# Conformer block on one core: attention outputs summed in two turns instead of in two banks with a reduce

## The chip, the cores and the metric

The kernel runs on one core of one Trainium2 chip. The metric is the device time of one execution in microseconds. PE is TensorE, the matrix engine, whose results land in PSUM (eight banks of 512 float32 for each of 128 partitions). ScalarE (ACT) computes functions such as the exponential, VectorE (DVE) does elementwise work and reductions, GpSimd (POOL) takes small work, and SP issues DMAs. Each engine works its own list of instructions in order, and the engines meet at semaphores: an instruction that waits holds everything behind it on its engine.

## The reference

Input x has 2 sequences of 4000 tokens with 144 features. One Conformer block is computed: a feed-forward half step, attention with 4 heads of 36 features, a gated convolution over 5 tokens, a second feed-forward half step, and a layer norm ahead of each part and at the end.

```
h = layernorm(x);  x = x + 0.5 * silu(h @ w_ff1a) @ w_ff1b
h = layernorm(x);  q, k, v = split(h @ w_qkv)                 # 4 heads of 36
p = softmax(q @ k.T * 36**-0.5);  x = x + (p @ v) @ w_o      # 4000 x 4000 for each head
h = layernorm(x) @ w_pw1;  h = h[:, :144] * sigmoid(h[:, 144:])
x = x + silu(conv5(h, dw)) @ w_pw2
h = layernorm(x);  x = x + 0.5 * silu(h @ w_ff2a) @ w_ff2b
return layernorm(x)
```

The attention is by far the most work: 2 x 4 heads x 4000 x 4000 exponentials, all of which have to leave PSUM through ScalarE or VectorE.

## The kernel before

Tokens are cut into 16 chunks of 512 (the last of each sequence has 416). The attention runs over 32 groups; a group is one chunk of queries and one pair of heads (`groups`). For each group there are 31 tiles of 128 keys, and a rest of 32 keys that is done for four heads at once (`rest`). A tile goes like this:

- Scores (`scores`): for both heads, and for each half of the 128 keys, one matmul on a 64 x 64 quadrant of PE. Four such matmuls run side by side and fill two banks. Two pairs of banks (0 to 3) take turns, so that the scores of a tile wait for the exponential of the tile two before.
- Exponential (`emit_exp`): one ScalarE instruction reads two banks and writes a PT buffer (1024 values a row, bf16). There are `NPT` PT buffers.
- Some tiles go to VectorE instead (`far_tiles`, and single heads in `emit_exp`): a linear instruction writes a 16-bit pattern to a PU buffer, and four more (`exact`, with the buffers PF and PC) correct it to an exponential. There are `NPD` PU buffers.
- Outputs (`outputs`, called by `emit_O`, `bits_outputs` and `rest`): for both heads and each half of the keys a quadrant matmul with the values (36 columns and a column of ones, which gives the softmax's denominator). The two halves of the keys sit on different row halves of PE and add into different banks: keys 0 to 63 of every tile into bank 4, keys 64 to 127 into bank 5, each for all 512 queries.
- At the end of a group the epilogue adds the two banks with one `tensor_reduce` on VectorE into the tile OTF (float32), PE transposes OTF, and VectorE divides. The first output of the next group has to wait until the banks are read.

Banks 6 and 7 are for everything else. While one group runs, the other parts of the block (layer norms, feed-forward, projections, convolution) of other chunks run between its tiles.

The order of the work is written by a planner in the kernel's Python code, at build time. `Rec` records every instruction with an estimated cost, keeps an estimated free time for each engine, and adds the latencies `LAT` from an instruction to the ones that need it. `Sched` holds threads (generators) which ask for an engine or a buffer; it runs the one that can start first, and among those within a tolerance the one with the best rank. The main loop at the end takes a thread or the next tile, whichever can start first. Numbers that steer it are in `TUNE`, one set for each eighth of the 32 groups: how free VectorE must be before it takes one head, how many tiles must be left before one goes to VectorE, how near GpSimd may be, the tolerance, and when a correction is hurried. `Rec.finish` turns the recorded dependences into semaphore waits. It leaves out dependences of PE on PE, as PE works in order.

All instructions are issued from one helper (line 163), so the profile's groups are told apart by the names of the tiles: PT, PU, PF, PC, OTF as above, QT and KT queries and keys, VA values, PS the PSUM banks, and DUM the zeros of filler matmuls.

Of the kernel before, what the change touches and what calls it, by code (L numbers as in the profile page):

```python
# [13 lines left out]
DH = 36  # L14
# [23 lines left out]
class Rec:  # L38
# [5 lines left out]
    LAT = dict(pe=0.195, act=0.243, dve=0.152, pool=0.08, sp=3.0)  # L44
# [14 lines left out]
    def op(self, eng, name, *a, r=(), w=(), q=None, cost=0.1, kind=None, lat=None, port=False, **k):  # L59
# [10 lines left out]
        for key in w:  # L70
            h = self.hist.setdefault(key, ([], []))
            o.deps += [(d, False) for d in h[0] + h[1] if d is not o]
            if h[1] and not (len(h[1]) == 1 and h[1][0] is o):
                self.hist[key] = ([o], [])
            else:
                h[0].append(o)
        start = self.free[eng]
        for d, raw in o.deps:
            if d.eng != eng or d.q is not None or (raw and eng != "pe"):
                start = max(start, d.done - self.NEAR.get((d.eng, eng), 0.0))  # L80
# [28 lines left out]
    def finish(self, group_qs=()):  # L109
        eng_clock = {e: {} for e in self.ENGS}  # L110
        for o in self.ops:
            clk = eng_clock[o.eng]
            need = {}
            for d, raw in o.deps:
                lane = d.eng if d.q is None else "q:" + d.q
                if d.q is None and d.eng == o.eng and (d.eng == "pe" or not raw or o.q is not None):
# [184 lines left out]
def bass_standalone__conformer_family_zipformer__speech_kernel(  # L301
# [35 lines left out]
    NPT, NPD, NUS, NQS = 7, 3, 7, 10  # L337
# [4 lines left out]
    TUNE = [(0.003, 10, 0.47, 0.032, 3), (0.003, 10, 0.47, 0.032, 3), (0.003, 10, 0.47, 0.032, 3), (0.025, 10, 0.56, 0.065, 3), (0.089, 13, 0.66, 0.057, 3), (0.003, 10, 0.47, 0.032, 3), (0.022, 10, 0.67, 0.039, 3), (0.075, 12, 0.7, 0.063, 3)]  # L342
# [30 lines left out]
    PF = sb("PF", [NPD, 2, CH], U16)  # L373
    PC = sb("PC", [NPD, 2, CH])
# [121 lines left out]
    def fill_start(until):  # L496
# [6 lines left out]
        Slots(R, range(n)) for n in (NXN, NXT, NTH, NTB, NHT, NSW, 2, 2, NPD))  # L503
    mode = {"front": True, "tail": False}
# [426 lines left out]
    an_of = {}  # L931

    def epilogue(b, qc, p, gi):
# [46 lines left out]
    def output_flags(gi, bk, hh):  # L980
        first = (gi, bk, hh) not in begun
        begun.add((gi, bk, hh))
        return dict(start=first, stop=o_left[gi] == 1, skip_group_check=True)

    def outputs(gi, terms, rk):

        n = wid(gi // 2)
        for t in range(max(map(len, terms))):
            for r, (m0, m1) in enumerate(halves):
                for hh in range(2):  # L990
                    if t < len(terms[hh]):
                        v, w = terms[hh][t]
                        op("pe", "matmul", PSV[64 * hh:64 * hh + DH + 1, 4 + r, 0:n], lhsT=v[m0:m1, 0:DH + 1],
# [321 lines left out]
```

## Time and profile before

| what | value |
|---|---|
| time, median of 3 runs | 934.28 us (934.25 to 934.55) |
| profiled execution, its time | 935.62 us |
| profiled execution, span from first to last instruction | 933.8 us |
| granted PE clock | 1.00 |
| exponential instructions on ScalarE (PT) | 848 |
| corrections on VectorE (PC from PF) | 155 |
| reduces into OTF | 32, 38.4 us |

The page's first part has the busy time of each engine. Its fifth part has the groups of instructions: how many, their busy time in all, the mean of one, and the idle time of the engine just before them with what ended it. The means of one instruction overlap with the next one's start, so start-to-start times from the timeline or the chain are shorter than they. The chain of work runs back from the last instruction to whatever released it, and so on; its shares say which engine set the pace.

### The profile page before, as it was taken

What the parts mean: (1) busy time and instruction counts of PE and PEld (TensorE: products, weight loads), DVE (VectorE), ACT (ScalarE), POOL (GpSimd) and SP (SyncE); (2) the same over time, 40 slices, a digit from 0 to 9 for tenths busy, and PEclk for the clock granted to TensorE, in tenths of its full rate; (3) what the DMA queues carried; (4) which work ended last, traced back from release to release, by engine and by line L of the source; (5) the groups of instructions that cost most, each with busy time, mean ns of one, the idle gap of its engine ahead of it and who ended that gap; (6) DMA issues with size and microseconds to landing.
All of it is one profiled execution on the core that took longest, in us unless ns stands there. A gap on an engine that the chain in (4) does not pass through costs nothing.

```text
span 933.8 us, 25544 instructions
## 1 busy us (share of the span) xinstructions
PE 860.8 (92%) x10838; PEld 343.0 (37%) x10838; DVE 858.4 (92%) x1975; ACT 884.2 (95%) x1126; POOL 170.8 (18%) x395
## 2 busy tenths in 40 slices
PE   8998899999999998999999999899988999899989
PEld 5633233333243333334343333333323333333447
DVE  8868999999999999999989999999999999898954
ACT  6799999999999999999999999999999999999963
POOL 7500010302111120211211111102202120130223
DMA  5310010103011020201100020101001020101100
GB/s 143 50 21 13 13 25 13 40 8 46 13 28 27 7 52 14 38 16 24 28 8 5 16 36 11 30 7 30 20 1 30 13 42 2 30 18 22 22 19 14
DMA packets 79810, 23.26 MB, mean 25 GB/s; under 512 B 77120, under 2 KB 79696, under 8 KB 79696
## 3 DMA queue, kind: packets, MB, share of 16 engines
q1 hardware_dynamic: 78656, 21.15, 11.6%
q8 instruction: 85, 1.39, 0.7%
q10 hardware_dynamic: 1040, 0.48, 0.2%
q14 instruction: 29, 0.24, 0.1%
HBM read 3.31 MB, written 2.30 MB: 6 GB/s over the span
## 4 chain that ended last, share of the span: by engine, by line
ACT 60%; PE 25%; DVE 13%; DMA 1%; issue 1%; POOL 1%; SPq 0%; ACTq 0%; DVEq 0%
ACT PT L163 52%; PE PS L163 25%; ACT TH L163 5%; DVE PU L163 4%; DVE PC L163 2%; DVE XN L163 1%; DVE ST L163 1%; DVE X L163 1%; ACT HT L163 1%; DVE HT L163 1%; DVE PF L163 1%; DVE OTF L163 1%; ACT PR L163 1%; DMA XT<-XN 0%; POOL RS L163 0%
## 5 line engine op out<-in xcount | busy, mean ns | idle before, releaser
L163 ACT ACTIVATE PT<-PS 128x1024 bf16<-128x1024 f32 (+2 forms) x848 | 795.8, 1067 | 9.7 <-PE PS L163 7.1
L163 PE MATMUL PS<-QT,KT 64*64 64x512 bf16 (+1 forms) x4032 | 431.1, 389 | 49.4 <-ACT PT L163 36.1
L163 PE MATMUL PS<-PT,VA 64*37 64x512 bf16 (+1 forms) x3350 | 327.1, 371 | 0.8 <-ACT PT L163 0.6
L163 PEld LDWEIGHTS PS<-QT,KT 64*64 64x64 bf16 x4032 | 128.2, 103 | 325.2 <-ACT PT L163 199.9
L163 DVE TENSOR_SCALAR PU<-PS 128x512 uint16<-128x512 f32 (+1 forms) x309 | 201.4, 671 | 5.8 <-PE PS L163 4.2
L163 POOL TENSOR_SCALAR RS<-ST 128x2 f32<-128x2 f32 (+1 forms) x160 | 33.2, 208 | 689.8 <-DVE ST L163 688.8
L163 POOL TENSOR_TENSOR RS<-RS,NHALF 128x2 f32<-128x2 f32 (+1 forms) x160 | 122.5, 766 | 13.3
L163 DVE TENSOR_TENSOR PC<-PC,PF 128x1024 bf16<-128x1024 bf16 (+1 forms) x155 | 103.4, 671 | 0.6
L163 DVE TENSOR_TENSOR PU<-PU,PC 128x1024 uint16<-128x1024 uint16 (+1 forms) x155 | 103.4, 669 | 0.2
L163 PEld LDWEIGHTS PS<-PT,VA 64*37 64x37 bf16 x3350 | 96.5, 96 | 13.5 <-ACT PT L163 1.3
L163 DVE TENSOR_SCALAR XN<-X,ST,RS 128x144 bf16<-128x144 bf16 (+1 forms) x312 | 83.2, 311 | 12.9 <-POOL RS L163 11.8
L163 ACT ACTIVATE TH<-PS 128x512 bf16<-128x512 f32 (+2 forms) x135 | 88.7, 657 | 1.9 <-PE PS L163 1.8
L163 PE MATMUL PS<-XT,WA 128*128 128x512 bf16 (+3 forms) x256 | 71.1, 378 | 6.7 <-DVE PU L163 3.4
L163 DVE BATCH_NORM_STATS2 ST<-X 128x6 f32<-128x288 bf16 (+1 forms) x160 | 69.1, 449 | 0.6 <-DMA X<-in_x_dram 0.3
L163 DVE SCALAR_TENSOR_TENSOR HT<-TH,PS 128x512 bf16<-128x512 bf16 (+3 forms) x105 | 64.8, 618 | 3.8 <-ACT TH L163 3.5
L163 PE MATMUL PS<-PU,VA 64*37 64x512 bf16 (+1 forms) x618 | 66.8, 376 | 1.1 <-DVE PU L163 0.8
L163 DVE SCALAR_TENSOR_TENSOR X<-PS,X 128x288 bf16<-128x288 f32 (+1 forms) x128 | 56.1, 450 | 9.9 <-PE PS L163 8.9
L163 DVE TENSOR_SCALAR PC<-PF 128x1024 bf16<-128x1024 uint16 (+1 forms) x155 | 63.0, 411 | 0.3
L163 DVE TENSOR_SCALAR PF<-PU 128x1024 uint16<-128x1024 uint16 (+1 forms) x155 | 62.5, 412 | 0.1
L163 PE MATMUL PS<-WB,HT 128*128 128x144 bf16 (+1 forms) x640 | 56.1, 228 | 2.0 <-ACT HT L163 0.6
L163 PEld LDWEIGHTS PS<-WB,HT 128*128 128x128 bf16 (+1 forms) x640 | 39.7, 101 | 35.3 <-issue 19.3
L163 DVE TENSOR_REDUCE OTF<-PS 128x512 f32<-128x1024 f32 (+1 forms) x32 | 38.4, 1199 | 12.6 <-PE PS L163 12.3
(97 smaller groups left out, 600.5 us busy)
## 6 DMA issues: line engine op xcount, KB each, us to landing
X<-in_x_dram SPq DMA_DIRECT2D x14, 144.0 KB, 3.7
out_dram<-XN SPq DMA_DIRECT2D x28, 72.0 KB, 1.8
XT<-XN SPq DMA_TRANSPOSE x94, 2.5
XT<-AN SPq DMA_TRANSPOSE x28, 2.5
X<-in_x_dram SPq DMA_DIRECT2D x2, 117.0 KB
out_dram<-XN SPq DMA_DIRECT2D x4, 58.5 KB
WA<-in_w_ff1a_dram ACTq DMA_DIRECT2D x1, 144.0 KB, 2.8
WB<-in_w_ff1b_dram ACTq DMA_DIRECT2D x1, 144.0 KB, 3.9
```

What stands on the lines that cost most here:

```text
L163: ins = getattr(eng, o.name)(*o.a, **o.k)
```

## The change

- An output matmul now takes 256 of the 512 queries. Bank 4 belongs to queries 0 to 255 and bank 5 to queries 256 to 511, and both halves of the keys add into the same bank. So that the two row halves of PE do not write the same bank together, the outputs of a tile come in two turns: in turn 0 the upper keys' row half works on the other bank than the lower keys' half, in turn 1 they swap (`a = r ^ ph`). Each turn has four matmuls of 256 columns in place of four of 512.
- A turn's first matmul waits by semaphore for the last matmul of the other turn (`sync`, which `finish` keeps although both are on PE). The turn may change only after scores or other work has come between (`may`, `turn`); where nothing else is left, a filler matmul is put in (`apart`). Tiles whose turn 0 is done are kept in the list `half`; several tiles can share a turn.
- The banks then hold whole sums, and the epilogue copies 512 values instead of reducing 1024. The epilogue is now a thread that asks for VectorE once the banks are ready, and the next group's outputs begin after the copy is recorded (`copied`).
- There are 8 PT buffers instead of 7, 4 PU buffers instead of 3, and 2 PF and PC buffers instead of 3, in a pool of their own (`pfp`).
- The planner's latencies and the eight sets in `TUNE` have other values.

```diff
-    LAT = dict(pe=0.195, act=0.243, dve=0.152, pool=0.08, sp=3.0)
+    LAT = dict(pe=0.214, act=0.254, dve=0.145, pool=0.08, sp=3.0)
...
-    NPT, NPD, NUS, NQS = 7, 3, 7, 10
+    NPT, NPD, NUS, NQS = 8, 4, 7, 10
+    NPF = 2
...
-    TUNE = [(0.003, 10, 0.47, 0.032, 3), (0.003, 10, 0.47, 0.032, 3), (0.003, 10, 0.47, 0.032, 3), (0.025, 10, 0.56, 0.065, 3), (0.089, 13, 0.66, 0.057, 3), (0.003, 10, 0.47, 0.032, 3), (0.022, 10, 0.67, 0.039, 3), (0.075, 12, 0.7, 0.063, 3)]
+    TUNE = [(0.013, 10, 0.53, 0.033, 2), (0.013, 10, 0.53, 0.033, 2), (0.013, 10, 0.53, 0.033, 2), (0.013, 10, 0.53, 0.033, 2), (0.05, 10, 0.68, 0.043, 3), (0.08, 12, 0.56, 0.04, 3), (0.013, 10, 0.53, 0.033, 2), (0.013, 10, 0.53, 0.033, 2)]
...
-        op("dve", "tensor_reduce", out=OTF[:, 0:n], in_=PSV[:, 4:6, 0:n].rearrange("p b n -> p n b"),
-           axis=mybir.AxisListType.X, op=ALU.add, r=[("ps", 4), ("ps", 5)], w=["OTF"],
-           cost=dve_cost(2 * n))
+        yield need("dve", rank=free_first)
+        op("dve", "tensor_copy", OTF[:, 0:n].rearrange("p (a n) -> p a n", a=2),
+           PSV[:, 4:6, 0:n // 2], r=["po"], w=["OTF"], cost=dve_cost(n))
+        copied[gi] = R.last
...
+    def may(ph):
+        return R.kind != "q" or turn[0] in (None, ph)
+
+    def outputs(gi, ph, terms, rk, rows=(0, 1)):
...
+        turn[0] = ph
+        other = last_out[1 - ph]
+        for r in rows:
+            m0, m1 = halves[r]
+            a = r ^ ph
+            for hh in range(2):
+                if terms[hh] is not None:
+                    v, w = terms[hh]
+                    last_out[ph] = op(
+                        "pe", "matmul", PSV[64 * hh:64 * hh + DH + 1, 4 + a, 0:n // 2], lhsT=v[m0:m1, 0:DH + 1],
+                        rhs=w[m0:m1, a * n // 2:(a + 1) * n // 2], r=rk, w=["po"],
+                        cost=0.107 / ((terms[0] is not None) + (terms[1] is not None)) / len(rows), kind="q",
+                        sync=other, **output_flags(gi, 4 + a, hh, ph))
+                    other = None
...
-            S.add(epilogue(*groups[gi], gi), first=True)
+            S.add(epilogue(*groups[gi], gi), R.ready("po"), first=True)
...
     def emit_pending(force=False):
-        while pend:
+        if half and may(1):
+            for m in half:
+                emit_O(m, 1)
+            half.clear()
+        while pend and may(0):
...
+            emit_O(m, 0)
+            half.append(pend.pop(0))
+
+    def apart():
+        if turn[0] is None or not banks.free:
+            return False
+        i = min(banks.free)
+        op("pe", "matmul", PSV[:, i, 0:128], lhsT=DUM[:, 0:128], rhs=DUM[:, 0:128], start=True, stop=True, r=["DUM"],
+           w=[("ps", i)], cost=0.058, kind="f")
+        turn[0] = None
+        return True
```

More of the change, by code (lines that the diff above doesn't have):

```diff
@@ L978, in bass_standalone__conformer_family_zipformer__speech_kernel, with output_flags @@
     begun = set()
-    def output_flags(gi, bk, hh):
+    def output_flags(gi, bk, hh, ph):
         first = (gi, bk, hh) not in begun
         begun.add((gi, bk, hh))
-        return dict(start=first, stop=o_left[gi] == 1, skip_group_check=True)
-    def outputs(gi, terms, rk):
-        n = wid(gi // 2)
[L988 to L993, printed above, removed]
-                           rhs=w[m0:m1, 0:n], r=rk, w=[("ps", 4 + r)], cost=0.0535 if all(terms) else 0.107,
-                           kind="q", **output_flags(gi, 4 + r, hh))
+        return dict(start=first, stop=ph == 1 and o_left[gi] == 1, skip_group_check=True)
+    turn = [None]
+    last_out = [None, None]
+    def may(ph):
+        return R.kind != "q" or turn[0] in (None, ph)
+    def outputs(gi, ph, terms, rk, rows=(0, 1)):
+        n = wid(gi // 2)
+        assert may(ph)
+        turn[0] = ph
[12 more added lines that the diff above has]
+                    other = None
     def output_done(gi, n=1):
@@ L1058, in begun_group @@
     def begun_group(gi):
[L1059 removed]
+        return any((gi, bk, hh) in begun for bk in (4, 5) for hh in range(2))
     def close_pair():
```

91 lines of the change are left out of this document (54 added, 37 removed).

## The prediction

> **What bounds the kernel now.** I read the page's table of engines, then the groups of instructions, then the chain of work, and for single handovers the timeline.
>
> ```profile
> span 933.8 us, 25544 instructions
> PE 860.8 (92%) x10838; PEld 343.0 (37%) x10838; DVE 858.4 (92%) x1975; ACT 884.2 (95%) x1126; POOL 170.8 (18%) x395
> q8 instruction: 85, 1.39, 0.7%
> ```
>
> This is the share of busy time over the whole span. Three engines are at 92 to 95%, so one more view is needed: the middle stretch alone, where attention runs, as busy time by engine.
>
> ```profile
> 75.00:890.00 815.00, 750.57 (x9580) 275.87 (x9578) 779.38 (x1730) 803.31 (x993) 128.22 (x290) 1.00 0.11 21
> ```
>
> From 75 to 890 us the columns are PE, weight loads, VectorE, ScalarE, GpSimd: ScalarE is busy 803.3 of 815 us (98.6%), VectorE 779.4 (95.6%), PE 750.6, with PE's clock granted in full (1.00). The chain of work of the same stretch says who sets the pace:
>
> ```profile
> by line: ACT PT L163 58.5%; PE PS L163 18.6%; ACT TH L163 6.1%; DVE PU L163 5.1%; DVE PC L163 2.1%; DVE XN L163 0.9%; issue 0.8%; DVE HT L163 0.8%; DVE PF L163 0.8%; DVE OTF L163 0.8%; DVE X L163 0.6%; ACT PR L163 0.6%; DVE ST L163 0.6%; DM
> ```
>
> The reader should see that the exponentials on ScalarE (PT) are most of it, that PE has 18.6% (152 of 815 us, in bursts), and that OTF, the work that the change replaces, has only 0.8% (6.5 us) itself. So little is gained directly. Indirectly more can be: the planner moves exponential tiles from ScalarE to VectorE as VectorE has room, so time freed on VectorE becomes time on ScalarE. These are the groups that this runs over:
>
> ```profile
> L163 ACT ACTIVATE PT<-PS 128x1024 bf16<-128x1024 f32 (+2 forms) x848 | 795.8, 1067 | 9.7 <-PE PS L163 7.1
> L163 PE MATMUL PS<-PT,VA 64*37 64x512 bf16 (+1 forms) x3350 | 327.1, 371 | 0.8 <-ACT PT L163 0.6
> L163 PE MATMUL PS<-PU,VA 64*37 64x512 bf16 (+1 forms) x618 | 66.8, 376 | 1.1 <-DVE PU L163 0.8
> L163 DVE TENSOR_SCALAR PC<-PF 128x1024 bf16<-128x1024 uint16 (+1 forms) x155 | 63.0, 411 | 0.3
> L163 DVE TENSOR_REDUCE OTF<-PS 128x512 f32<-128x1024 f32 (+1 forms) x32 | 38.4, 1199 | 12.6 <-PE PS L163 12.3
> ```
>
> **Term 1, the reduce becomes a copy.** The reduce reads two banks (1024 values a row); the copy reads 512 and writes the same 512 float32. There is no such copy in the trace; the nearest rows move 512 or 416 float32 values of PSUM to SBUF.
>
> ```profile
> L163 DVE TENSOR_REDUCE OTF<-PS 128x512 f32<-128x1024 f32 x28 | 34.3, 1224 | 8.2 <-PE PS L163 8.0
> L163 DVE CAST KT<-PS 128x512 bf16<-128x512 f32 x25 | 17.2, 686 | 6.6 <-PE PS L163 6.6
> L163 DVE CAST QT<-PS 128x416 bf16<-128x416 f32 x4 | 2.3, 584 | 0.0
> L163 DVE TENSOR_REDUCE OTF<-PS 128x416 f32<-128x832 f32 x3 | 3.1, 1025 | 0.8 <-PE PS L163 0.8
> ```
>
> 28 x (1224 - 686) + 4 x (1025 - 584) ns = 15.1 + 1.8 = 16.8 us of VectorE less. Only the output type differs (bf16 in the row); I take the row.
>
> **Term 2, VectorE's wait before it.** The old reduce is put into VectorE's order as soon as the last output matmul is planned, and VectorE stands 12.6 us in all before it. In the new code the epilogue is a thread that becomes ready when the planner holds the banks for done, and other VectorE work can be put ahead. In the middle stretch it looks like this (us in total, times, longest):
>
> ```profile
> DVE OTF L163 <- PE PS L163: 8.8, 24, 0.7
> ```
>
> The other 3.5 us of the page's 12.3 are one wait at the end of the last group, where VectorE has nothing to put ahead. Bounds: 0 to 9.1 us given back; I take 6, as the waits are short and regular, of a kind that the planner's times resolve. Terms 1 and 2 together: 22.8 us of VectorE (bounds 16.8 and 25.9).
>
> **Term 3, what that buys.** One tile that moves takes from ScalarE one exponential and gives VectorE six instructions. Busy means overlap, so I take start-to-start steps, from the chain in order of time:
>
> ```profile
> 399.23 6.42 ACT PT L163 x7
> 418.40 1.20 DVE PU L163 x2
> 419.60 0.34 DVE PC L163
> 419.93 0.33 DVE PF L163
> 420.26 0.60 DVE PC L163
> 420.86 0.60 DVE PU L163
> ```
>
> ScalarE: 6.42 / 7 = 0.917 us a tile. VectorE: 1.20 + 0.34 + 0.33 + 0.60 + 0.60 = 3.07 us (the two conversions, the two tensor_scalars, the product and the sum). With both engines ending together, 22.8 us free let x tiles move with 3.07x + 0.917x = 22.8: x = 5.7, and ScalarE's end comes 5.2 us earlier. With 16.8 us it is 4.2 tiles and 3.9 us, with 25.9 us 6.5 tiles and 6.0 us; if none move, 0. I take 5.2. The more PU buffers (3 to 4) let a fourth such tile be open; PF and PC drop from 3 to 2, which costs nothing as VectorE runs one such chain at a time or two.
>
> **Term 4, the handover between groups.** The next group's first output must wait for the banks to be read. In the timeline of one handover (start, us, engine):
>
> ```profile
> 404.12 0.45 PE L163 MATMUL PS<-PT,VA 64*37 64x512 bf16 x4
> ...
> 404.62 1.23 DVE L163 TENSOR_REDUCE OTF<-PS 128x512 f32<-128x1024 f32 x1 [0.35 <-PE PS L163]
> ...
> 405.94 0.60 PE L163 MATMUL PS<-PT,VA 64*37 64x512 bf16 x8
> ```
>
> The last outputs start at 404.12 and the next ones at 405.94; between them stands the 1.23 us reduce. A 0.69 us copy takes 0.54 us off; against that the last tile's second turn comes one score step later. I book the direct part only: OTF's 0.8% of the chain is 6.5 us, of which 0.54/1.23 would go, 2.9 us; half of it is lost to the second turn: 1.4 us. One more PT buffer (7 to 8) only makes up for tiles held longer between their two turns; ScalarE's 7.1 us of waits on PE before PT are all that it could win or double. I book 0 (bounds -3 to +7).
>
> **Term 5, PE's price.** Output matmuls go from 512 to 256 columns: 3350 + 618 = 3968 become 7936, so the 992 sets of four become 1984 sets; the 32-row rest goes from 64 to 128. The columns streamed stay the same. What a step of a short set costs beyond streaming is seen in the convolution's quadrant matmuls:
>
> ```profile
> 400.20 0.41 PE L163 MATMUL PS<-QT,KT 64*64 64x512 bf16 x4
> 400.44 0.39 PE L163 MATMUL PS<-PT,VA 64*37 64x512 bf16 x4
> 400.66 0.38 PE L163 MATMUL PS<-QT,KT 64*64 64x512 bf16 x2
> ...
> 303.42 0.60 PE L163 MATMUL PS<-UA,DG 64*64 64x384 bf16 x8
> ```
>
> ```profile
> L163 PE MATMUL PS<-UA,DG 64*64 64x256 bf16 x112 | 12.1, 272 | 0.0
> ```
>
> From 400.44 to 400.66 a set of 512 columns takes 0.22 us, so 768 columns should take 0.33. By the code the eight convolution matmuls are four pairs of 384, 128, 256 and 256 columns. The last pair lasts 0.27 us, so the three steps before it, 768 columns, take 0.60 - 0.27 = 0.33 us: no overhead within the 0.03 us of rounding. A step costs at most 0.01 us beyond its columns, and I take that: 992 more steps, 10 us of PE. [...]
>
> Then the new wait. Before each change of turn PE waits for its own last output matmul of the other turn. The trace has no wait of PE on PE. From below it is 0: a set of scores lies between the turns, and PE often stands before those scores anyway, long enough for any matmul to end:
>
> ```profile
> PEld PS L163 <- ACT PT L163: 201.2, 425, 1.3
> ```
>
> From above: the outputs at 404.12 last 0.45 us where a set lasts 0.39, so the last of them began at some 404.18, and the waiting reduce started at 404.62, 0.44 us on. The columns take 0.22 us, so completion trails them by 0.22. A set of scores between hides that (0.24 us, 400.20 to 400.44); without one, all 0.22 is lost. I take 0.02 us, the 0.41 against 0.39 us that a set takes when its weights were not loaded ahead; about one turn per ScalarE tile, 848 x 0.02 = 17 us. Behind a waiting output on PE stand the next scores, and behind those the next exponential. PE's 10 + 17 = 27 us count where PE is in the chain, 18.6%: 5.0 us. But a third of the turns follow a score set that waited (425 of some 848 half, of which the chain's PE bursts have fewer), so I book 3.5 (bounds 1.9 and 848 x 0.22 x 0.186 + 1.9 = 36.6). Where nothing else is left, a filler matmul parts the turns:
>
> ```profile
> L163 PE MATMUL PS<-DUM 128*128 128x128 bf16 x254 | 16.7, 219 | 0.0
> ```
>
> That is 0.22 us at most; one at each of 32 group ends would be 7 us of PE, 1.3 us by its share, booked at 0.
>
> Changed planner numbers (latencies, the eight TUNE sets) alter the order everywhere; the trace can't price that, and the handful of us that PE's and POOL's waits of 7 to 12 us suggest go into the range both ways. SP's and POOL's queues get nothing new. The instruction stream grows by 4000 matmuls and their weight loads; its queue now takes 0.7% of the DMA engines, so a third more is booked at 0.
>
> **Sum.** -5.2 - 1.4 + 3.5 = -3.1 us. The profiled execution took 935.62 us around its 933.8 us span, 1.3 us above the median of 934.28; the sum goes onto the median: 931.2.
>
> **The rivals.**
> A. The forecast: VectorE's freed time becomes 4 to 7 tiles, PE gives back some. 931.2, own range 926 to 932.4. Chance 0.40.
> B. PE doesn't mind at all, since its waits for ScalarE are long (201 us), and the better handover and fourth PU buffer fill ScalarE's remaining 12 us of idle time by half: -6.0 - 2.9 - 6 = -15 at most, -10.5 at half of the last two: 919 to 926. For it: ScalarE has the 7.1 us of waits on PE. Against: it is at 98.6% already. Chance 0.18.
> C. The freed time isn't used: tiles move only where PE, two free banks and a PU buffer allow it, so the count stays near 155 and VectorE simply idles more. Then -1.4 + 3.5: 932.4 to 936.2. For it: VectorE already idles 36 us of the 815. Chance 0.15.
> D. The other side: the turn change becomes PE's bound. Place: the bursts where PE is in the chain, when PE comes to the second turn before the first one's matmuls have landed, and the next scores queue behind it. Price 848 x t x 0.186. It decides where it eats the 6.6 us of terms 3 and 4 less the 1.9 of the steps: t = 4.7 / 158 = 0.030 us; at the middle of the bounds, 0.1 us, it is 15.8 us: 934.3 - 6.6 + 1.9 + 15.8 = 945.4. For it: 75 to 890 us PE is busy 92%. Against: scores between the turns. 936.2 to 950, chance 0.27.
>
> **The numbers.** A measurement of this kernel can tell about 0.2% (1.9 us) from no change. Faster (below 932.4): A and B, 0.58. Within: C, 0.15. Slower: D, 0.27. Predicted is A's 931.2. The range 921 to 943 leaves out B's best and D's worst, about 2 in 10; since it holds both signs, A's own range stands beside it above.
>
> **What would show it.** Right: no reduce but 32 copies into OTF at 0.66 to 0.70 us, idle before them under 6 us; PC<-PF up from 155 to 159 to 162 and PT down from 848 by as many; output matmuls near 7936 with idle time before them of a few us; ScalarE still 98% or more in the middle. Wrong, by D: a row of PE waiting on PE of tens of us, PE's share of the chain above 25%, and ScalarE's waits on PE well over 7.1 us. By C: PC<-PF near 155 with VectorE's busy time 17 us lower. By B: ScalarE's idle time in the middle under 7 us.

## The result, and the profile after

| | kernel before | changed kernel |
|---|---|---|
| median of 5 runs | 934.55 us (934.25 to 935.78) | 938.88 us (937.08 to 940.18) |
| ratio, 95% interval | | 1.0041 (1.0029 to 1.0053): slower |
| profiled execution, its time / its span | 935.62 / 933.8 us | 937.08 / 935.3 us |
| PT instructions / corrections PC from PF / into OTF | 848 / 155 / 32 reduces | 845 / 160 / 32 copies |

The forecast was 931.2 us with 0.58 on faster. The direction was wrong, though most of the counts came out as forecast (PT fell by three only, as single heads moved too). First the changed kernel's page, its table of engines:

```profile
span 935.3 us, 33695 instructions
PE 871.4 (93%) x14891; PEld 450.0 (48%) x14891; DVE 859.7 (92%) x2009; ACT 882.4 (94%) x1123; POOL 164.5 (18%) x395
```

ScalarE is 1.8 us less busy than before (884.2), and the span is 1.5 us longer: ScalarE idles 3.3 us more. The groups that the forecast named, from the same page:

```profile
L165 ACT ACTIVATE PT<-PS 128x1024 bf16<-128x1024 f32 (+2 forms) x845 | 790.1, 1045 | 10.2 <-PE PS L165 6.4
L165 PE MATMUL PS<-PT,VA 64*37 64x256 bf16 (+1 forms) x6660 | 326.1, 268 | 1.7 <-DVE OTF L165 1.1
L165 PEld LDWEIGHTS PS<-PT,VA 64*37 64x37 bf16 x6660 | 175.5, 96 | 90.2 <-PE PS L165 21.8
L165 PE MATMUL PS<-PU,VA 64*37 64x256 bf16 (+1 forms) x1276 | 92.7, 270 | 1.5 <-DVE PU L165 1.5
L165 DVE TENSOR_SCALAR PC<-PF 128x1024 bf16<-128x1024 uint16 (+1 forms) x160 | 64.7, 411 | 0.6
```

The copies stand in the view of groups with their forms put together:

```profile
L165 DVE COPY OTF<-PS 128x512 f32<-128x512 f32 (+1 forms) x32 | 21.4, 670 | 0.4 <-PE PS L165 0.3
```

6660 + 1276 = 7936 output matmuls, 32 copies, five more corrections; VectorE's idle time before OTF fell from 12.6 to 0.4 us. What this bought is asked of the middle stretch, 75 to 890 us (columns as in the prediction: PE, weight loads, VectorE, ScalarE, GpSimd):

```profile
75.00:890.00 815.00, 760.05 (x13492) 378.41 (x13493) 778.85 (x1763) 802.18 (x990) 120.71 (x288) 1.00 0.11 22
```

VectorE's busy time is what it was (779.4, now 778.9), and so is its idle time. The copies' 17.0 us became tiles, but the 12.2 us that it no longer waits before OTF did not: it now waits elsewhere. PE is 9.5 us busier. The chain of work of the same stretch:

```profile
by line: ACT PT L165 44.3%; PE PS L165 22.0%; DVE PU L165 9.6%; DVE PC L165 4.9%; ACT TH L165 4.2%; DVE XN L165 1.9%; DVE PF L165 1.8%; DVE HT L165 1.7%; DVE X L165 1.1%; DVE ST L165 0.9%; POOL RS L165 0.8%; issue 0.8%; DVE OTF L165 0.7%; D
```

The exponentials fell from 58.5 to 44.3% of it. PE rose from 18.6 to 22.0%, and VectorE's tiles (PU and PC) from 7.2 to 14.5%: the three engines now hand the pace to each other. The waits of the same stretch (us in all, times, longest):

```profile
PEld PS L165 <- ACT PT L165: 131.5, 333, 1.3
...
PEld PS L165 <- PE PS L165: 25.3, 107, 0.4
...
DVE X L165 <- PE PS L165: 8.1, 15, 1.4
ACT PT L165 <- PE PS L165: 6.4, 21, 0.6
```

PE waiting on PE is new, 25.3 us. `DVE X` waiting on PE is where VectorE's stall went: this row was small before. The same view of the kernel before:

```profile
PEld PS L163 <- ACT PT L163: 191.8, 407, 1.3
...
DVE X L163 <- PE PS L163: 1.5, 3, 1.2
```

Last, the body of the attention, from the first start of a PT instruction to the last, as the view of one tile gives it (shortest, median, longest duration, then first and last start). Before:

```profile
L163 ACT ACTIVATE PT<-PS x848: 512/1056/1347, 47.2 to 895.8; 128x1024 bf16<-128x1024 f32 x146, 128x832 bf16<-128x832 f32 x22, 128x512 bf16<-128x512 f32 x2
```

After:

```profile
L165 ACT ACTIVATE PT<-PS x845: 517/1042/1367, 48.1 to 895.6; 128x1024 bf16<-128x1024 f32 x144, 128x832 bf16<-128x832 f32 x19, 128x512 bf16<-128x512 f32 x5, 128x416 bf16<-128x416 f32 x1
```

The body is 848.6 us before and 847.5 after, 1.1 shorter. It begins 0.9 later, and from the last PT start to the end of the span there are 39.7 us instead of 38.0, 1.7 more. The sum, +1.5 us, is the difference of the two spans. The medians differ by 4.3 us. The other 2.8 lie between the executions: the changed kernel's profiled one is 1.8 us under its median, the one before 1.1 above its own. So single executions differ by as much as the body gained, and body times are good to about 1 us.

### The profile page after: what moved, and what is told of

It reads as the page before. It is cut to its first block, busy times and chain, and to the rows that moved or that the text cites. A ratio compares the mean times of both kernels' runs of the same rounds, so it can differ in the third digit from the quotient of the medians.

```text
span 935.3 us, 33695 instructions
## 1 busy us (share of the span) xinstructions
PE 871.4 (93%) x14891; PEld 450.0 (48%) x14891; DVE 859.7 (92%) x2009; ACT 882.4 (94%) x1123; POOL 164.5 (18%) x395
## 4 chain that ended last, share of the span: by engine, by line
ACT 45%; PE 28%; DVE 24%; POOL 1%; issue 1%; DMA 1%; SPq 0%; ACTq 0%; DVEq 0%
ACT PT L165 39%; PE PS L165 28%; DVE PU L165 8%; DVE PC L165 4%; ACT TH L165 4%; DVE XN L165 2%; DVE PF L165 2%; DVE HT L165 2%; DVE X L165 1%; POOL RS L165 1%; DVE ST L165 1%; ACT HT L165 1%; DVE OTF L165 1%; DVE QT L165 0%; ACT PR L165 0%
## 5 line engine op out<-in xcount | busy, mean ns | idle before, releaser
L165 PE MATMUL PS<-QT,KT 64*64 64x512 bf16 (+2 forms) x4032 | 429.8, 389 | 41.8 <-ACT PT L165 28.2
L165 PE MATMUL PS<-PT,VA 64*37 64x256 bf16 (+1 forms) x6660 | 326.1, 268 | 1.7 <-DVE OTF L165 1.1
L165 PEld LDWEIGHTS PS<-QT,KT 64*64 64x64 bf16 (+1 forms) x4032 | 127.6, 103 | 236.5 <-ACT PT L165 134.9
L165 PEld LDWEIGHTS PS<-PT,VA 64*37 64x37 bf16 x6660 | 175.5, 96 | 90.2 <-PE PS L165 21.8
L165 DVE TENSOR_SCALAR PU<-PS 128x512 uint16<-128x512 f32 (+1 forms) x319 | 207.8, 670 | 8.0 <-PE PS L165 5.9
L165 POOL TENSOR_TENSOR RS<-RS,NHALF 128x2 f32<-128x2 f32 (+1 forms) x160 | 118.5, 741 | 13.3
L165 DVE TENSOR_TENSOR PU<-PU,PC 128x1024 uint16<-128x1024 uint16 (+1 forms) x160 | 106.8, 670 | 0.2
L165 PE MATMUL PS<-PU,VA 64*37 64x256 bf16 (+1 forms) x1276 | 92.7, 270 | 1.5 <-DVE PU L165 1.5
L165 PEld LDWEIGHTS PS<-PU,VA 64*37 64x37 bf16 x1276 | 40.6, 96 | 21.9 <-issue 7.6
L165 PEld LDWEIGHTS PS<-WB,HT 128*128 128x128 bf16 (+1 forms) x640 | 39.8, 101 | 21.4 <-issue 10.9
## 6 DMA issues: line engine op xcount, KB each, us to landing
out_dram<-XN SPq DMA_DIRECT2D x4, 58.5 KB
```

The source lines that it names most:

```text
L165: ins = getattr(eng, o.name)(*o.a, **o.k)
```

## The experiments

The expectations name theories by numbers. Theory 1: the body gains what was forecast, and PE's price eats it, by the waits (1a) or by the steps (1b). Theory 2: VectorE's time is worth little, and the order with its two ends decides. Theory 3: the order that the turns force loses by itself. Theories 4 and 5 came later: PE's amount of work limits along with ScalarE and VectorE (4), or only the latency from one engine to the next does (5). All ratios are to the kernel before, run beside each (its medians: 934.67, 934.84, 935.05 and 934.69 us).

| kernel | median, us | ratio (95%) |
|---|---|---|
| before_copy | 932.62 | 0.9975 (0.9965 to 0.9985) |
| before_split | 937.75 | 1.0034 (1.0021 to 1.0046) |
| before_wait | 935.09 | 1.0003 (0.9994 to 1.0012) |
| after_nowait | 937.41 | 1.0021 (1.0012 to 1.0031) |
| after_alt | 935.07 | 1.0008 (0.9999 to 1.0017) |
| after_whole | 951.74 | 1.0186 (1.0172 to 1.0200) |
| after_oldplan | 953.39 | 1.0195 (1.0180 to 1.0211) |
| before_tuned | 931.08 | 0.9961 (0.9949 to 0.9974) |
| after_tuned | 940.94 | 1.0068 (1.0055 to 1.0080) |
| copy_tuned | 930.33 | 0.9949 (0.9937 to 0.9961) |
| thread_tuned | 929.50 | 0.9946 (0.9933 to 0.9958) |
| before_half | 930.33 | 0.9947 (0.9933 to 0.9960) |

### One part at a time in the old order

The copy alone, with the planner's cost kept, so that the order is the old one:

```diff
-        op("dve", "tensor_reduce", out=OTF[:, 0:n], in_=PSV[:, 4:6, 0:n].rearrange("p b n -> p n b"),
-           axis=mybir.AxisListType.X, op=ALU.add, r=[("ps", 4), ("ps", 5)], w=["OTF"],
+        op("dve", "tensor_copy", OTF[:, 0:n].rearrange("p (a n) -> p a n", a=2),
+           PSV[:, 4:6, 0:n // 2], r=[("ps", 4), ("ps", 5)], w=["OTF"],
            cost=dve_cost(2 * n))
```

> The kernel before, in its old order, with the reduce of two banks replaced by a copy of 256 values from each bank, so the second half of the keys' sums is left out for each query and the output is that of half the keys. It prices the cheaper VectorE instruction alone, without the planner using the freed time. Theory 1 (the body gains what the forecast said and PE's new steps and waits eat it): 0.54 us less VectorE in each of 32 groups, but no tile moves, so 1 to 5 us faster through shorter handovers. Theory 2 (VectorE's freed time is worth nothing; only planner order and the ends decide): within 1 us of before.

Measured: 0.9975, 2.3 us faster (1.4 to 3.3). With no tile moved, this is what a 0.5 us shorter handover is worth.

The output matmuls split alone (two of 256 columns into the bank that the one of 512 had, no waits):

```diff
+            for a in range(2):
                 for r, (m0, m1) in enumerate(halves):
...
-  op("pe", "matmul", PSV[..., 4 + r, 0:n], ..., rhs=w[m0:m1, 0:n], ...)
+  op("pe", "matmul", PSV[..., 4 + r, a * n // 2:(a + 1) * n // 2], ..., rhs=w[m0:m1, a * n // 2:(a + 1) * n // 2], ...)
```

> The kernel before, in its old order, with each output matmul split into two of 256 columns into the same bank, no turns and no new waits. It prices the doubled number of output matmuls alone. Theory 1: 992 more steps of up to 0.01 us, 10 us of PE, 2 us slower. Theory 2 (steps are free, the loss lies in the order of the work): within 1 us of before. [...]

Measured: 1.0034, 3.2 us slower (2.0 to 4.3). Its group of output matmuls:

```profile
L163 PE MATMUL PS<-PT,VA 64*37 64x256 bf16 (+1 forms) x6700 | 329.4, 267 | 0.8 <-ACT PT L163 0.6 <-DVE OTF L163 0.2
```

One lasts 267 ns, against 371 for 512 columns: the matmuls are as much shorter as their columns are fewer, and hardly any PE time is added. From start to start a set of four with 256 columns takes 109 ns at the median (110 at the mean), where a set of 512 takes 216, so a step costs 1 to 2 ns beyond its columns. For 992 sets that is 1 to 2 us of PE. Most of the 3.2 us must be something else, and where they arise was not settled.

PE's wait alone: the first outputs after each set of scores wait by semaphore for the last outputs before it.

```diff
+        other = last_out[0] if turn[0] is None else None
+        turn[0] = 0
...
-                        op("pe", "matmul", PSV[...], ..., kind="q", **output_flags(gi, 4 + r, hh))
+                        last_out[0] = op("pe", "matmul", PSV[...], ..., kind="q", sync=other, **output_flags(gi, 4 + r, hh))
+                        other = None
```

> The kernel before, in its old order, with a wait of PE for its own last output matmul ahead of the first outputs after each set of scores; matmuls stay at 512 columns. It prices the turn's wait alone (the wait is a little longer here, as 512 columns land later than 256). Theory 1: 0.02 us for each of some 850 waits, 17 us of PE, 2 to 4 us slower. Theory 2: hidden by the scores between, within 1 us of before.

Measured: 1.0003, no difference. Its waits in the middle stretch:

```profile
PEld PS L165 <- ACT PT L165: 184.5, 390, 1.1
...
PEld PS L165 <- PE PS L165: 25.9, 91, 0.5
```

The row of PE waiting on PE is as long as the changed kernel's, and it cost nothing that can be measured: a part of it took the place of waits for ScalarE (191.8 us before, 7.3 less here), and the rest did not reach the end. Theory 1a falls for the old order.

### The changed kernel's order, with PE's price taken out

The order written by the planner is kept to the instruction. First without the waits: row half r always writes bank 4 + r, so nothing has to wait.

```diff
-  PSV[64 * hh:64 * hh + DH + 1, 4 + a, 0:n // 2]
+  PSV[64 * hh:64 * hh + DH + 1, 4 + r, a * n // 2:(a + 1) * n // 2]
...
-  if d.q is None and d.eng == o.eng and raw != "sync" and (d.eng == "pe" or not raw or o.q is not None):
+  if d.q is None and d.eng == o.eng and (d.eng == "pe" or not raw or o.q is not None):
```

> The changed kernel in its own order, instruction for instruction, but each row half of PE adds into its own bank again (as before), so that no wait between the turns is needed and none is in the program. The epilogue's copy then takes 256 queries of one half of the keys from each bank, so half of the keys' sums is left out of the output. It prices the turn's waits alone, inside the changed order. Theory 1a (the waits are what costs): 3 to 8 us faster than the changed kernel. Theory 1b (the doubled matmuls cost, the waits are hidden, as in the run that added waits to the old kernel): within 1.5 us of the changed kernel.

Measured: 1.0021. Against the change's 1.0041 the waits cost 0.20%, 1.9 us (0.4 to 3.3), in this order. That lies between the two theories.

Then without the splits too: each tile's outputs are whole, 512 columns, in one of its two turns (even tiles in turn 0, odd ones in turn 1).

```diff
-  PSV[64 * hh:64 * hh + DH + 1, 4 + a, 0:n // 2], ... rhs=w[m0:m1, a * n // 2:(a + 1) * n // 2]
+  PSV[64 * hh:64 * hh + DH + 1, 4 + r, 0:n], ... rhs=w[m0:m1, 0:n], ghost=ph != par
```

(`ghost`: in the plan, not in the program. `par` is the tile's parity.)

> The changed kernel in its own order, where each tile's outputs are done whole in one of its two turns (512 columns, each row half into its own bank, tiles of even number in turn 0, of odd number in turn 1) and nothing in the other turn. So PE's work is spread over the turns as in the changed kernel, but there are neither doubled matmuls nor waits between turns. Half of the keys' sums is left out of the output. It mends the run that did all in turn 0 and so held the scores back. Theory 1b (steps and waits cost what they cost alone: 3.0 and 0.5 to 1.5 us): 934 to 936. Theory 3 (the order is what loses): 937 to 939.

Measured: 1.0008, as Theory 1b expected. So PE's whole price in this order is 1.0041 - 1.0008, 0.33% or 3.1 us (1.7 to 4.5). What is left is the copies, the thread, the moved tiles and the new order, and it is not faster than the kernel before. Its body:

```profile
L179 ACT ACTIVATE PT<-PS x845: 518/1058/1360, 48.2 to 893.4; 128x1024 bf16<-128x1024 f32 x144, 128x832 bf16<-128x832 f32 x19, 128x512 bf16<-128x512 f32 x5, 128x416 bf16<-128x416 f32 x1
```

845.2 us, 3.4 shorter than before and 2.3 shorter than with the turns. But the ends keep their price: 1.0 us at the front, and 39.8 us after the last PT start (933.2 - 893.4) instead of 38.0.

A first version of this, with all outputs of 512 columns in turn 0 and none in turn 1, changed one thing more, as the turns were no longer alike:

```diff
-  rhs=w[m0:m1, a * n // 2:(a + 1) * n // 2], r=rk, w=["po"],
+  rhs=w[m0:m1, 0:n], r=rk, w=["po"], ghost=ph,
```

> As the run without waits, and the output matmuls are 512 columns wide again: turn 0 does all 512 queries, turn 1 is left out of the program, and the order of everything else is that of the changed kernel. Half of the keys' sums is left out of the output here too. It prices waits and steps together. Theory 1b: 3 us faster than the changed kernel, as splitting cost the old kernel 3.1 us. Theory 3 (what loses is the order itself: outputs held back to a second turn, a slower front and a longer end): within 1.5 us of the changed kernel, with the end still some 38.8 us after the last exponential.

Measured: 1.0186. Its waits in the middle stretch:

```profile
ACT PT L173 <- PE PS L173: 17.0, 47, 1.0
```

The block of turn 0 is twice as long, and ScalarE waits 17.0 us for PE instead of 6.4. It says nothing on the steps. It fits that the longer block holds the next scores back, and so that the place of PE's work counts for more than its amount, but no run shows this by itself.

### The planner's numbers

The changed kernel with the LAT and TUNE lines of the kernel before:

```diff
-    LAT = dict(pe=0.214, act=0.254, dve=0.145, pool=0.08, sp=3.0)
+    LAT = dict(pe=0.195, act=0.243, dve=0.152, pool=0.08, sp=3.0)
...
-    TUNE = [(0.013, 10, 0.53, 0.033, 2), (0.013, 10, 0.53, 0.033, 2), ...
+    TUNE = [(0.003, 10, 0.47, 0.032, 3), (0.003, 10, 0.47, 0.032, 3), ...
```

> The changed kernel with the latencies and TUNE sets of the kernel before. Theory 1 (structure costs PE time): 937 to 943, near the changed kernel, as the structure is the same. Theory 2 (the order that the planner's new numbers give is what loses): clearly away from the changed kernel's 938.9, 935 or less if the new numbers are worse, above 943 if they are what the structure needs.

Measured: 1.0195, 14.5 us more than with its own numbers, part of it with a lower granted clock (0.991 to 0.995). Then the kernel before with nothing but its TUNE chosen anew, by the planner's own estimate of the end:

```diff
-    TUNE = [(0.003, 10, 0.47, 0.032, 3), (0.003, 10, 0.47, 0.032, 3), (0.003, 10, 0.47, 0.032, 3), (0.025, 10, 0.56, 0.065, 3), ...
+    TUNE = [(0, 10, 0.47, 0.005, 3), (0, 10, 0.461, 0.032, 4), (0, 10, 0.47, 0.032, 3), (0.034, 10, 0.47, 0.055, 3), (0, 10, 0.47, 0.046, 3), (0, 10, 0.436, 0.046, 2), (0.034, 10, 0.467, 0.022, 3), (0.059, 10, 0.451, 0.018, 4)]
```

> The kernel before with TUNE sets chosen anew in the same manner as for the runs with the planned epilogue, and nothing else. It tells how much of the gain of those two runs is the choice of TUNE. If all of it: 929 to 931. If the planned epilogue is what gains: 932 to 934.

Measured: 0.9961, 3.6 us faster with no other edit. And the changed kernel with its TUNE chosen in the same manner:

```diff
-    TUNE = [(0.013, 10, 0.53, 0.033, 2), (0.013, 10, 0.53, 0.033, 2), (0.013, 10, 0.53, 0.033, 2), ...
+    TUNE = [(0.013, 10, 0.478, 0.005, 3), (0.013, 10, 0.478, 0.005, 3), (0, 10, 0.478, 0.005, 3), (0.013, 10, 0.478, 0.005, 3), (0.013, 10, 0.478, 0.005, 3), (0.013, 10, 0.478, 0.005, 3), (0.03, 11, 0.478, 0.005, 4), (0.013, 10, 0.558, 0.005, 4)]
```

> The changed kernel with TUNE sets chosen anew in the same manner, and nothing else. If the change's own structure is what loses, it stays behind the kernel before: 935 to 938. If it was only badly tuned: under 933.

Measured: 1.0068, slower than with the numbers it came with. But a stall of 4.2 us is in it, and a granted clock of 0.995 in four of the five runs. Three windows of 3.4 us at half clock make such a clock, and by 1.6 us each (last section) they are an estimated 4.8 us. Together that is up to some 9 us of 940.9, so this run does not tell whether the change was badly tuned. The planner's estimate did not carry over to the chip here. The planner's numbers move the kernel before by 3.6 us and the changed one by 14.5. Each term of the prediction's sum is of the size of the former or little larger, and none comes near the latter.

### The copy and the thread without the turns

Both kernels keep the old outputs and let the planner place the epilogue:

```diff
+    copied = {-1: 0.0}
...
+        yield need("dve", rank=free_first)
         op("dve", "tensor_reduce", out=OTF[:, 0:n], ...)
+        copied[gi] = R.last
...
-            S.add(epilogue(*groups[gi], gi), first=True)
+            S.add(epilogue(*groups[gi], gi), max(R.ready(("ps", 4)), R.ready(("ps", 5))), first=True)
...
-                t = max(t, R.ready("OTF"))
+                if gi - 1 not in copied:
+                    return
+                t = max(t, copied[gi - 1])
```

`thread_tuned` keeps the reduce and computes the whole output. In `copy_tuned` the reduce is the copy of before_copy, with its own cost of `dve_cost(n)`. TUNE is chosen anew in both, in the manner of before_tuned; thread_tuned's is

```
TUNE = [(0.003, 10, 0.56, 0.021, 4), (0.033, 10, 0.47, 0.034, 4), (0.033, 10, 0.47, 0.026, 4), (0.033, 10, 0.56, 0.021, 4),
        (0.033, 10, 0.47, 0.026, 4), (0.033, 10, 0.47, 0.026, 4), (0.033, 10, 0.428, 0.017, 5), (0.056, 9, 0.19, 0.034, 5)]
```

> The kernel before with the changed kernel's epilogue (a thread that asks for VectorE when the banks are ready, and a copy in place of the reduce, so half of the keys' sums is left out of the output), no turns, 512 columns, and TUNE sets chosen anew for it. It tests the gain that was forecast, terms 1 to 4 without PE's price. Theory 1: 934.5 - 6.6 = 928, with 3 to 7 corrections more than 155. Theory 2 (VectorE's time is worth little): 932 to 934.

> The kernel before with the epilogue as a thread that asks for VectorE when the banks are ready; the reduce stays, the output is whole; TUNE sets chosen anew for it. It prices term 2, VectorE's wait before the reduce. Theory 1: 6 us of VectorE are worth 1.4 us by moved tiles, so some 933, and idle time before the reduce under 5 us. Theory 2: no change, 934 to 935.

Measured: 0.9949 and 0.9946. Against before_tuned's 0.9961 that is 0.12 and 0.15%, 1.1 and 1.4 us, inside what the intervals can tell. VectorE's groups into OTF, before_tuned:

```profile
L163 DVE TENSOR_REDUCE OTF<-PS 128x512 f32<-128x1024 f32 (+1 forms) x32 | 38.4, 1199 | 11.2 <-PE PS L163 10.7
```

thread_tuned:

```profile
L163 DVE TENSOR_REDUCE OTF<-PS 128x512 f32<-128x1024 f32 (+1 forms) x32 | 38.2, 1195 | 1.6 <-PE PS L163 1.5
```

copy_tuned, with its corrections:

```profile
L163 DVE COPY OTF<-PS 128x512 f32<-128x512 f32 (+1 forms) x32 | 21.6, 675 | 2.3 <-PE PS L163 2.3
...
L163 DVE TENSOR_SCALAR PC<-PF 128x1024 bf16<-128x1024 uint16 (+1 forms) x162 | 66.4, 416 | 0.5
```

The thread takes the wait before OTF away (11.2 to 1.6 us) without any copy. The copy frees another 16.6 us, corrections go from 156 (before_tuned) to 162, and the time stays. By the shortest start-to-start steps of an exponential (0.904 us for 1024 values, 0.744 for 832, 0.477 for 512, 0.397 for 416) copy_tuned's PT instructions are 4.6 us less work than before_tuned's. Its body is 1.1 us shorter, from 843.2 to 842.1. before_tuned:

```profile
L163 ACT ACTIVATE PT<-PS x844: 512/1072/1408, 46.8 to 890.0; 128x1024 bf16<-128x1024 f32 x146, 128x832 bf16<-128x832 f32 x21, 128x512 bf16<-128x512 f32 x1, 128x416 bf16<-128x416 f32 x1
```

copy_tuned, with the chain of its middle stretch:

```profile
L163 ACT ACTIVATE PT<-PS x847: 512/1057/1370, 46.6 to 888.7; 128x1024 bf16<-128x1024 f32 x142, 128x832 bf16<-128x832 f32 x19, 128x512 bf16<-128x512 f32 x7, 128x416 bf16<-128x416 f32 x2
...
by line: ACT PT L163 44.6%; PE PS L163 22.6%; DVE PU L163 9.4%; ACT TH L163 4.5%; DVE PC L163 4.3%; DVE HT L163 1.9%; DVE XN L163 1.8%; DVE PF L163 1.5%; POOL RS L163 1.2%; DVE ST L163 1.0%; DMA XT<-XN 1.0%; DVE X L163 1.0%; issue 0.7%; DVE
```

This is the clean form of the question that Term 3 answered, without turns or splits: even so only a quarter of the work that ScalarE loses shows in the body, in single executions. One window at half clock lies in copy_tuned's (903.6 to 907.0 us), but behind the body. The chain is spread over the three engines as the changed kernel's is (before_tuned's has PT at 58.4% and PE at 19.7%), so the spread needs no turns.

The medians came out as Theory 2 says, but not at one clock. Four of copy_tuned's five runs had 0.996, three of before_tuned's and of thread_tuned's had 1.000. The few runs at 0.998 took 928.9 us (copy_tuned, one run), 931.1 and 931.3 (thread_tuned), 931.1 and 933.0 (before_tuned). So the freed time may be worth some 3 us that the clock takes back, which five runs of each cannot settle. Theory 1's 928 for copy_tuned and Theory 2's 932 to 934 both missed its 930.3, as neither counted the 3.6 us of new TUNE sets. thread_tuned is faster than the kernel before and the changed one, by 5.0 us of the former.

copy_tuned also bears on theory 3. It and after_alt do the same kinds of work: a planned epilogue, the copy, whole outputs of 512 columns. They differ in the order (after_alt's was written for the turns and with the change's numbers) and in the number of PT, PU, PF and PC buffers. Between them lie 0.59%, 5.5 us. So the order that came with the change loses 5.5 us against a newly chosen one; what the turns' rule, the numbers and the buffers each have in it is not told apart, and after_tuned cannot tell it. The kernel before has its own 3.6 us of this, by before_tuned, so against its order 1.9 us are left, beside PE's 3.1.

### Half of PE's outputs away

To tell whether PE's amount of work holds the others, the output matmuls of every second ScalarE tile are left out, in the old order:

```diff
-                 [("PT", n % NPT), ("VA", b * CPB + kt // NB), "VA1"])
+                 [("PT", n % NPT), ("VA", b * CPB + kt // NB), "VA1"], ghost=n % 2 == 1)
```

> The kernel before in its own order, with the output matmuls of every second ScalarE tile left out of the program (so some 3350 / 2 = 1675 matmuls fewer, and the output lacks those keys). It asks whether ScalarE's lost time in the attention, some 36 us beyond the unhindered steps of its exponentials, is time that PE takes. Some 420 sets of 0.22 us are 92 us of PE less. Theory 4 (PE bounds together with ScalarE, so freed ScalarE time turns into waits on PE): at least 8 us faster, 927 or less, with ScalarE's waits on PE before PT well under 7 us. Theory 5 (the loss is latency from exponential to score to exponential and not PE's load): within 3 us of before.

Measured: 0.9947, 5.0 us faster. The chain of the middle stretch:

```profile
by line: ACT PT L177 63.4%; PE PS L177 9.5%; ACT TH L177 6.5%; DVE PU L177 4.4%; DVE PC L177 2.7%; DMA XT<-AN 1.5%; DVE XN L177 1.3%; DMA XT<-XN 1.0%; DVE X L177 1.0%; DVE ST L177 1.0%; DVE HT L177 0.9%; DVE OTF L177 0.9%; DVE QT L177 0.8%;
```

PE's share halved, to 9.5%. By its old share (18.6%) the 9.1 points should give 74 us of a chain; 5 came, so the chain's share of an engine is no price for its work. But this kernel also ran at a lower granted clock in all six runs (0.991 to 0.994), which takes part of the gain back. By its mean clock of 0.993 its profiled execution has some four windows at half clock (last section), by 1.6 us each an estimated 6.4 us; at the full clock it would be some 11 us faster, as Theory 4 asks. Theory 4's other sign is missing: ScalarE's waits on PE before PT are 6.4 us, hardly under 7.1. So theories 4 and 5 stay open.

## Why the prediction was wrong

**Term 1, right.** 38.4 - 21.4 = 17.0 us less, 16.8 booked; 683 ns for a copy of 512 values where the row of KT had 686.

**Term 2, right in kind, and empty.** 12.2 us of waits before OTF went, more than the upper bound of 9.1, as the long wait at the end of the last group went too. But VectorE's busy time in the middle did not rise. The time reappears as other waits, `DVE X` on PE first (1.5 to 8.1 us). That VectorE "can put other work ahead" held; that this work is then additional did not. In thread_tuned it did: there VectorE is busy 790.0 us of the middle against before_tuned's 784.4, with two corrections more and 1.4 us less work of PT, what the forecast gives for 6 us.

**Term 3, the tiles right, their worth wrong.** Corrections rose by five, 5.7 forecast, and by the shortest steps the PT instructions are 4.6 us less work (725, 102, 15 and 6 of 1024, 832, 512 and 416 values before; 715, 105, 23 and 2 after), 5.2 forecast. The body is only 1.1 us shorter, no more than single executions differ by. The step that failed is "with both engines ending together ... ScalarE's end comes 5.2 us earlier": it takes ScalarE as always ready to go on. ScalarE's steps grew longer instead, by 4.6 - 1.1 = 3.5 us: 2.3 of it goes with PE's splits and waits (after_alt's body is that much shorter), and 1.2 stays without them. In copy_tuned against before_tuned, with no turns at all, 3.5 of 4.6 us of the body are lost in the same way. ScalarE at 98.6% busy in the middle looked like the one bound. But a tile that goes to VectorE still needs the same matmuls, and its scores and outputs may then come in VectorE's rhythm; that this is what lengthens ScalarE's steps was not tested and stays open.

**Term 4.** The copy in the fixed order gave 2.3 us, 1.4 booked (all of the direct part is 2.9).

**Term 5, right in size.** 3.1 us against 3.5: after_alt 1.0008, after_nowait 1.0021, after 1.0041. How it splits is not settled: in the old order the steps alone cost 3.2 us and the waits 0.3, in the new one 1.2 and 1.9, each give or take more than a microsecond. PE waited 26.2 us for itself in the whole span, 17 booked:

```profile
PEld PS L165 <- PE PS L165: 26.2, 109, 0.4
```

The steps were taken at up to 10 ns beyond their columns, 1.9 us in the sum. In before_split they cost 1 to 2 ns, so less than was taken; the split alone still cost 3.2 us.

**The order and its ends, not priced.** The prediction put the planner's numbers only into the range, as "the handful of us", so the sum had no term for the order. The new order costs 2.6 us at the two ends, 0.9 at the front and 1.7 at the end. The end of the attention before, on ScalarE:

```profile
893.57 3.31 ACT L163 ACTIVATE PT<-PS 128x832 bf16<-128x832 f32 x4
```

and on VectorE:

```profile
897.34 1.02 DVE L163 TENSOR_REDUCE OTF<-PS 128x416 f32<-128x832 f32 x1 [3.50 <-PE PS L163]
```

The last exponential ends at 896.88 and the reduce starts 0.46 us later. After, on ScalarE, PE and VectorE:

```profile
893.39 3.13 ACT L165 ACTIVATE PT<-PS 128x832 bf16<-128x832 f32 x4
```

```profile
896.78 0.61 PE L165 MATMUL PS<-XT,WA 128*128 128x512 bf16 x2
897.32 0.45 PE L165 MATMUL PS<-PT,VA 64*37 64x208 bf16 x12
897.79 0.61 PE L165 MATMUL PS<-XT,WA 128*128 128x512 bf16 x2
898.33 0.27 PE L165 MATMUL PS<-PU,VA 64*37 64x208 bf16 x4
898.80 0.61 PE L165 MATMUL PS<-XT,WA 128*128 128x512 bf16 x2 [0.20 <-DVE HT L165]
899.34 0.27 PE L165 MATMUL PS<-PU,VA 64*37 64x208 bf16 x4
```

```profile
899.67 0.58 DVE L165 COPY OTF<-PS 128x416 f32<-128x416 f32 x1
```

The exponential ends at 896.52 and the copy starts 3.15 us later. The last turns are parted by matmuls of the second feed-forward (XT, WA), of half a microsecond each, where the prediction had a filler of 0.22 us at a group's end, booked at 0. The epilogue of the last group stands alone behind this. Of the 2.7 us by which the copy comes later, 1.7 reach the end of the span.

**The account.** Terms 3 and 4 were to give 6.6 us; without PE's price (after_alt) the change stands 0.7 us above the kernel before (-0.1 to 1.6). In the profiled executions after_alt's body is 3.4 us shorter and its ends are 2.8 longer, 0.6 us faster in all; from there to 0.7 slower is the 1.3 us by which these executions lie away from their medians. So two steps failed together: the moved tiles did not become time in full, and the order with its ends, which had no term, took what they gave. PE's price comes on top. Part of that price is the clock: the changed kernel's median run had a granted clock of 0.998, the kernel before's 1.000. At 1.000 alone the changed kernel's two runs are at 937.1 and 937.4 us, after_alt at 935.0 and the kernel before at 934.6. There the change loses 2.6 us instead of 4.3, and PE's price is 2.2.

**The rivals.** D named the right side, and the result lies in its stretch (936.2 to 950) and in the whole range, 6.5 us under its own 945.4. Half of its mechanism was right: the row of PE on PE is there, in tens of us. But its other two signs are not (22.0% of the chain where it asked for over 25, ScalarE's waits on PE 6.4 us where it asked for well over 7.1), and before_wait shows that such a row can cost nothing. A had the counts. C said that the freed time isn't used; its sign, corrections near 155, is not there, but the outcome is: the tiles moved, and in the profiled executions three quarters of what they took from ScalarE came back as longer steps. B's PE that doesn't mind was wrong by the 3.1 us.

## What to carry to other kernels

Where two or three engines are each over 90% busy, work taken from the busiest need not become time: here the body gained 1.1 us of 4.6, and the same in the cleaner pair, with an uncertainty of about 1 us. Price a change of an order written by a planner as order first: give the old kernel newly chosen numbers too, since that alone was worth 3.6 us, most of the 5.0 that the best version gained. A long row of an engine waiting is not a cost until a kernel without the wait is faster, and the end of the last group, where nothing else covers it, deserves a term of its own.

## What had not been expected of the hardware

**Half-clock stretches in the middle of dense work.** Of 61 runs of the kernel before, 48 had a mean granted clock of 1.000 and a median of 934.6 us, and 13 had 0.998 and 936.2. In before_half the stretch can be seen. Three windows in a row, with PE's busy time and matmuls first and the granted clock third from the end:

```profile
663.30:666.70 3.40, 1.90 (x22) 0.61 (x22) 3.37 (x8) 3.40 (x5) 0.00 (x0) 1.00 0.02 6
666.71:670.10 3.39, 3.18 (x30) 1.18 (x27) 3.11 (x8) 2.58 (x4) 1.76 (x4) 0.50 0.09 21
670.13:673.50 3.37, 3.19 (x38) 1.18 (x36) 2.90 (x9) 3.19 (x5) 0.00 (x0) 1.00 0.00 0
```

After 3.4 us in which PE was busy 1.90 us, the clock is 0.50 for the next 3.4, and then 1.00 again. PE was not idle ahead of it: it had matmuls in flight for 56% of the first window. Each half-clock window goes with about 1.6 us (936.2 - 934.6). As an estimate from these lines, 3.4 us at 0.50 take 1.7 us of full clock out of 934, 0.0018 of the mean, so a clock of 0.998, 0.996, 0.995 or 0.993 stands for one, two, three or four of them.

Seven of the fourteen profiled executions have a mean clock under 1.000: 0.998 in before_copy, before_wait, copy_tuned and thread_tuned, 0.995 in after_oldplan and after_tuned, 0.993 in before_half. In before_copy the clock is 0.51 from 671.90 to 675.30 us, behind 6.85 us in which PE was busy for 5.25. But PE is busy for only 1.92 of the 3.41 us from 671.00 in the kernel before, and for 1.85 of the 3.41 us from 47.30 in the changed kernel, and there the clock is 1.00 in these and in the next 3.41 us. So PE's busy time in a stretch does not decide it alone, and what else does was not shown. By the mean clocks, such stretches came in all six runs of before_half, in all of after_tuned and copy_tuned, and in three of the changed kernel's five, but in one of before_wait's eleven. So a few us of gain from lighter PE work can be lost to the clock (an estimated 6.4 us in before_half). What makes one order leave such windows more often than another was not tried.

**GpSimd copies that last as long as VectorE's corrections.** In after_tuned two small copies on GpSimd stand ahead of the convolution. In the timeline, GpSimd:

```profile
182.46 3.74 POOL L165 COPY UA<-UA 128x2 bf16<-128x2 bf16 x1 [4.88 <-DVE UB L165]
186.13 0.18 POOL L165 COPY UB<-UB 128x1 bf16<-128x1 bf16 x1
```

VectorE in the same time, and then PE:

```profile
182.91 0.76 DVE L165 TENSOR_SCALAR PF<-PU 128x1024 uint16<-128x1024 uint16 x2
183.59 0.76 DVE L165 TENSOR_SCALAR PC<-PF 128x1024 bf16<-128x1024 uint16 x2
184.26 1.29 DVE L165 TENSOR_TENSOR PC<-PC,PF 128x1024 bf16<-128x1024 bf16 x2
185.46 0.69 DVE L165 TENSOR_TENSOR PU<-PU,PC 128x1024 uint16<-128x1024 uint16 x1
```

```profile
186.37 0.64 PE L165 MATMUL PS<-UA,DG 64*64 64x512 bf16 x2 [4.16 <-POOL UB L165]
```

A copy of two values a row took 3.74 us while VectorE ran a chain of corrections from SBUF to SBUF without a gap, and ended when that chain did; the next such copy took 0.18. In the kernel before, the 28 copies into UA take 0.19 us at the median and 3.50 at the longest; the longest starts at 818.33 us, and VectorE runs corrections without a gap from 817.95 to 821.77. In after_tuned PE stood 4.16 us behind the 3.74 us copy, with the next scores queued. PE's window before 185.4 us was thus almost empty (0.25 us busy), and the clock was 0.50 for the next 6.8 us: one stall cost twice. The 3.74 us span about seven VectorE instructions in a row; that these are what held the copy was not tested.
